# Re-ordering the first five steps of a fused delta-rule and MLP kernel by a new hand-written instruction order

## The chip, the cores and the metric

The kernel runs on one core of a Trainium2 chip. The metric is the device time of one execution in microseconds (us). Inside the core, TensorE (PE, with its weight loads listed apart as PEld), VectorE (DVE), ScalarE (ACT) and GpSimd (POOL) each run their own instructions strictly in the order in which the program issues them, and SyncE (SP) issues nearly all DMAs, also in order.

## The reference

The first part is a delta-rule recurrence over 768 tokens, for 4 batches and 8 heads of width 48; its output is turned into 3072 rows of 384 and goes through an MLP with a hard-swish:

```python
k_n = k / (np.linalg.norm(k, axis=-1, keepdims=True) + 1e-06)
for t in range(S):
    kt, vt, bt = (k_n[:, :, t], v[:, :, t], beta[:, :, t, None])
    y[:, :, t] = np.einsum('bhd,bhde->bhe', q[:, :, t], state)
    v_old = np.einsum('bhde,bhd->bhe', state, kt)
    state = state + bt[:, :, :, None] * np.einsum('bhd,bhe->bhde', kt, vt - v_old)
# x: y as (B*S, H*D) = (3072, 384)
h = x @ w_in                                  # w_in 384 x 2048
g = h * np.clip(h + 3.0, 0.0, 6.0) / 6.0
out = g @ w_out                               # w_out 2048 x 384
```

q, k, v and beta are float32; the two weight matrices are float64 and have to be made float32 on the chip.

## The kernel before

**Tiling.** The 768 tokens are cut into 24 chunks of 32 tokens, called steps 0 to 23; a chunk of all four batches fills 128 partitions. Two steps make one MLP block of 256 rows, so there are 12 blocks. Within a step, the recurrence inside the chunk is solved with the inverse of a triangular 32x32 matrix for each batch and head; between steps a state of 48x48 for each batch and head is carried on. Step 0 gets its inverse by seven small products on PE (`product`); steps 1 to 4 get theirs together by a substitution on DVE (`halves_of`, which loads the matrices in another layout from DRAM and writes the result back through DRAM) and a join on PE (`join`); steps 5 to 8 come from one longer substitution (`inverse`), and so on.

**Weights.** Each matrix is loaded in 8 pieces of 768 KB, 16 pieces in all, as raw float64 words. For each piece ACT computes the exponent in four passes (`scales`, line 335) and DVE builds the float32 in three operations (`convert`, lines 357, 362 and 368). Pieces 1 to 8 are `w_in`, 9 to 16 `w_out`. The raw pieces pass through a few homes, so a late piece waits until an earlier one has been read.

**Steps 0 to 4 and blocks 0 and 1** follow `ORDER`, a text of 822 words. `do` takes one word after the other and issues the next piece of the generator that the word names; this fixes the order on every engine. From step 5 on a loop with a fixed plan issues the rest.

What the words issue:

| word | what one word issues | engine |
|---|---|---|
| `k`, `q`, `v` | one load of 48 KB (one batch of one step) | SP |
| `w` | one raw weight piece, 768 KB | SP |
| `a`; `c` | one of the four ACT passes of a piece; one of its three DVE operations | ACT; DVE |
| `n0` `n1` `n2` `n4` `n5` `n9` | norms of the keys of the steps from that one on (square, sum, root, reciprocals) | ACT, DVE |
| `m`, `b` | beta mask of a step; keys times beta | POOL |
| `p` | preparation of a step, 7 words: scaled keys (POOL), transposes of k (PE), their copy (ACT), transposes of q (PE), their copy (ACT), scores `sc` (PE), masked scores `LB` (DVE) | several |
| `l` | masked scores of a step to DRAM, for the substitution | SP |
| `x0` | the 16 parts of step 0's inverse | PE, DVE, ACT |
| `x1` to `x4` | the 6 parts of a join | several |
| `i1`, `i2` | the substitution of steps 1 to 4 (35 words: load of `A`, 28 DVE operations, a memset, a store, 4 loads back) and of steps 5 to 8 (66 words) | SP, DVE |
| `h` | the chain of a step: state products `ks` (PE), `R` (DVE), `pz` (PE), `Z` (ACT), `su` (PE), new state (DVE); step 0 has only the last four | several |
| `y` | the output of a step: `y`, `py`, `yt`, and at last `xT` (ACT), the MLP's input | several |
| `ua`, `ub` | one of 16 chunks of the up-product of half of block 0 (rows of step 0; of step 1) | PE |
| `ra` `ga`, `rb` `gb`, `ru` `gu` | ACT and DVE part of the hard-swish of such a chunk | ACT, DVE |
| `u` | one unit of MLP work: of every four, two are down-products of block 0 and two are up-products of block 1; the last four are down-products of block 1 | PE |
| `e`, `z`, `s`, `B` | output, settings, pads, beta loads | several |

Four PSUM tiles (`psM`) are shared in turn by `pt`, `pi`, `pz`, `py`, `yt`, `ph` and `po`, so a product waits until the tile four places earlier has been read by ACT or DVE. Two larger ones (`psC`) hold `sc`, `ks` and `su`. There are three `vf` buffers for values, two `kf` buffers for keys (one for a group of four steps) and four for queries.

Below, "the fifth `c`" is the fifth time that this word occurs.

Of the kernel before, what the change touches and what calls it, by code (L numbers as in the profile page):

```python
# [19 lines left out]


ORDER = """
k*2 z k*2 B*2 k B*2 w q s*2 q n0 s q n0 s q z n0 s q s*2 k s z m0 k z*3 n0 k a c m1 k a k c q s a
q*2 n0 n1 n0 q n0 p0 a n1 k*2 b0 p0 n1 c k*2 p0*2 k n1 k n1 p0 n1*2 w p1 n2 p0 w n2 b1 k p1 p0 k*2
x0 p1 m2 p1 k n2 q p1 q n2 x0*2 n2 p1 q a n2 c n2 x0 n2*2 a c p2 a b2 p2 q*2 p3 a q*2 x0 b3 p3 n4
q c p2 q p2 p3 q n4 x0 p2 q c q n4 p2 a n4 w n4*2 p3 n4 w p2 p4 a w x0 w b4 p4 p3 k c x0 p4 m3 k a
k*2 a p1 p4 p3 p4 l2 x0 m4 a c a c a l1 p4 p3 a x0 p4 m5 a c l3 m6 a*2 c a l4 c k x0 c a k*2 x0 n5
k c x0 a k n5 a v x0 a c x0 v c a v x0 a i1 c v a v c w n5 c w a v n5 w c k*2 i1 h0 i1 k i1*2 h0 k
i1*2 y0 i1*3 h0 y0 i1*2 k a y0 i1 c i1 y0 i1 a c a k i1*2 k h0 a i1 h1 a i1 c a k i1 k ua i1 y1 v
c n5 v i1*2 ua ra v y1 a q i1 q i1 ua ga ra q i1 a i1 ua q ga i1*2 q ua ra i1 n5 x1 x2 i1 ra x3 ua  # L30
ga x4 ra q ga n5 ga ua q h1 ra q ua ra q a ua q ga*2 ua q ra n5 ra q ua ra ga i1 ga n5 ua ga ra i1
c a i1 ua i1 ga ua ra c q ra ua ra q a c q k ga a x1 ua k ga*2 x1 ra k x2 ra ga x2 x1 k u x2 x3 k
ga x1 k c k x2 x1 k n5 n9 n5*2 k c v*2 n5 x4 x3 p5 x2 v n9 v h1 p6 x3 n9 v*2 n9 b6 k b5 k w*2 v p5
h1 v n9 v y1 p7 p5 n9 v*2 p6 y1 b7 k*2 c a y1 p8 c h1 y1 b8 p6 p8 a p7 w x3 h1 w a k a k*2 h2 x3 c
k p7 k ub p8 h2 k p8 rb ub y2 k p8 gb c ub rb c a h2 gb rb y2 ub h2 k a gb k ub k ub rb k rb gb h2
v rb gb a gb v k ub h2 a w k ub rb c k ub a k h3 gb k rb c k rb gb a ub v gb c v y2 rb a gb ub y2
w a h3 ub rb ub rb gb v rb gb ub a v gb c ub v rb v h3 rb gb c a ub gb c h3 y2 rb u y2 gb y3 p6 a
y3*2 p6 h3 y3 a y3 h3 p5 y3 q p5 u c q n9 q a c u q c q ru q a gu p5 q n9 q ru p6 p5 a u p6 m7 l5
a gu l6 u a c m8 a p7 u q p7 c q c a q p7 q ru a p8 p7 u p8 m9 l7 n9 c l8 u ru m10 u gu*2 n9*2 u
n9*2 p9 i2 u ru b9 gu p10 p9 ru u b10 p9 gu p9 i2 x4 p9 i2*3 u i2*2 x4 i2 u i2*4 x4 i2 ru i2*2 h4  # L40
x4 gu i2 u y4 i2 h4 u ru i2*2 y4 u i2*2 u gu i2*3 u ru i2 gu i2 u ru i2 gu i2 u i2*3 u i2*3 h4 ru
i2 gu p9 h4 i2*2 y4 p9 u i2 p11 l9 y4 u ru i2 y4 gu u y4 i2*3 u i2*4 u ru i2 gu i2 u ru i2*3 gu u
i2*4 u e i2*2 e*2 i2*3 u ru i2*2 gu i2 h4 ru e gu p10 h4 u p10*2 u p10 u i2*3 p10 u p10 l10
"""


# [1286 lines left out]
```

## Time and profile before

| | |
|---|---|
| median of three runs | 698.09 us (697.37 to 699.77) |
| the profiled execution's own time | 701.2 us |
| its span, first to last instruction | 699.5 us |
| PE busy | 651.9 us, 93% of the span |
| DVE, ACT, POOL busy | 440.0, 240.6, 93.5 us |
| mean granted PE clock | 0.959 of full speed |

The profiled execution took 701.2 us, 1.7 us more than its span and 3.1 us more than the median. A predicted difference is worked out on the profiled execution and then taken from the median.

The page cuts the span in 40 slices of 17.5 us and gives the busy share of each engine in tenths. Above the slices stand the totals; the "chain that ended last" follows the work back from the end; the groups list instructions by line; the list of waits says which engine stood idle until which instruction of another engine was done.

### The profile page before, as it was taken

The page shows a single profiled execution, that of the slowest core. Times are in us where ns is not written, and L with a number is a line of the kernel's source. Part 1 is how long each engine was busy: PE and PEld are TensorE (multiplying, and loading weights), DVE is VectorE, ACT ScalarE, POOL GpSimd, SP SyncE. Part 2 cuts the span into 40 slices and gives each one's busy share as a digit, 9 for nine tenths or more (in the row PEclk, how much of TensorE's full clock was granted, in tenths as well). Part 3 has the DMA queues.
Part 4 walks back from the last instruction along what each step waited for, and adds up shares of the span by engine and source line. Part 5 has one row for each costly group of instructions (what it writes and reads, how often), then busy time and mean ns, then how long its engine had stood idle before and what let it go on. Part 6 is the DMA issues. An engine that isn't in the chain of part 4 may idle for free.

```text
span 699.5 us, 25481 instructions
## 1 busy us (share of the span) xinstructions
PE 651.9 (93%) x11208; PEld 570.9 (82%) x11208; DVE 440.0 (63%) x1174; ACT 240.6 (34%) x476; POOL 93.5 (13%) x146
## 2 busy tenths in 40 slices
PE   2637779999999999999999999999999999999997
PEld 2437669777668998998998998988988989989997
DVE  5678737878545797653796743895544984545342
ACT  5786448722213313313213213223223132132230
POOL 7520110321321010411100401100000000000000
PEclk9857859999999999999999999999999999999999
DMA  6787777401513123414113422015130014000000
GB/s 134 213 195 196 115 210 173 67 33 20 104 39 80 34 43 70 48 39 88 32 29 78 45 45 65 10 42 78 18 70 2 2 36 59 16 11 1 24 0 23
DMA packets 137999, 45.27 MB, mean 65 GB/s; under 512 B 128192, under 2 KB 131264, under 8 KB 137888
## 3 DMA queue, kind: packets, MB, share of 16 engines
q1 hardware_dynamic: 137632, 43.35, 30.3%
q8 instruction: 88, 1.44, 0.9%
q10 hardware_dynamic: 256, 0.30, 0.2%
q14 instruction: 23, 0.19, 0.1%
HBM read 32.87 MB, written 10.75 MB: 62 GB/s over the span
## 4 chain that ended last, share of the span: by engine, by line
PE 81%; DVE 9%; DMA 4%; SPq 3%; issue 2%; ACT 1%; POOL 0%; DVEq 0%
PE ph L946 34%; PE po L1052 23%; PE po L987 6%; PE ks L775 3%; PE pt L474 3%; PE pz L796 3%; PE su L892 2%; PE py L796 2%; PE sc L495 2%; DVE A L724 2%; DVE pr L719 2%; SPq L147 2%; DVE g L1038 1%; DMA qb<-in_q_dram 1%; PE yt L841 1%
## 5 line engine op out<-in xcount | busy, mean ns | idle before, releaser
L946 PE MATMUL ph<-xT,w_in 128*128 128x256 f32 (+1 forms) x1248 | 269.5, 370 | 1.9 <-DVE g L958 1.7
L946 PEld LDWEIGHTS ph<-xT,w_in 128*128 128x128 f32 x1248 | 221.0, 193 | 31.3 <-DVE g L958 2.8
L955 ACT ACTIVATE t<-ph,halves 128x256 f32<-128x256 f32 (+1 forms) x208 | 94.5, 457 | 202.2 <-PE ph L946 201.0
L958 DVE SCALAR_TENSOR_TENSOR g<-t,ph 128x256 f32<-128x256 f32 (+1 forms) x208 | 81.9, 398 | 124.7 <-ACT t L955 124.4
L1052 PE MATMUL po<-w_out,g 128*128 128x192 f32 x640 | 113.3, 328 | 0.0
L1052 PEld LDWEIGHTS po<-w_out,g 128*128 128x128 f32 x640 | 103.8, 190 | 0.5
L1052 PE MATMUL po<-spare,g 128*128 128x192 f32 x480 | 84.8, 330 | 0.0
L1052 PEld LDWEIGHTS po<-spare,g 128*128 128x128 f32 x480 | 78.1, 190 | 1.8
L1038 DVE TENSOR_TENSOR g<-g 128x256 f32<-128x256 f32 x160 | 65.5, 462 | 0.5 <-PE po L1052 0.5
L724 DVE TENSOR_TENSOR A<-A,pr 128x30 f32<-128x30 f32 (+19 forms) x150 | 52.6, 351 | 3.7
L335 ACT ACTIVATE spare<-spare,places 128x768 uint16<-128x768 uint16 (+1 forms) x56 | 52.5, 941 | 4.1 <-DMA qb<-in_q_dram 2.3
L719 DVE TENSOR_TENSOR pr<-A 128x30 f32<-128x30 f32 (+19 forms) x150 | 49.7, 331 | 2.9
L423 POOL TENSOR_TENSOR mb<-beta_tok,mask 128x256 f32<-128x256 f32 x48 | 35.8, 769 | 104.0 <-DVE LB L505 103.9
L987 PE MATMUL po<-w_out,g 128*128 128x384 f32 x128 | 46.4, 501 | 0.0
L1059 ACT ACTIVATE o<-po 128x192 f32<-128x192 f32 x40 | 13.2, 331 | 88.5 <-PE po L1052 82.2
L482 ACT ACTIVATE KQ<-pt 128x512 f32<-128x512 f32 x48 | 28.5, 595 | 31.7 <-PE pt L474 30.4
L458 POOL TENSOR_TENSOR kb<-kf,inv 128x384 f32<-128x384 f32 x24 | 21.3, 888 | 113.4 <-PE pt L474 76.8
L845 ACT ACTIVATE xT<-yt 128x384 f32<-128x384 f32 x24 | 11.7, 488 | 64.7 <-PE yt L841 64.7
L987 PEld LDWEIGHTS po<-w_out,g 128*128 128x128 f32 x128 | 23.4, 192 | 12.6 <-issue 0.5
L474 PE MATMUL pt<-ident,kb 128*128 128x128 f32 x96 | 18.6, 328 | 15.8 <-POOL kb L458 15.8
L775 PEld LDWEIGHTS ks<-state,KQ 64*64 64x64 f32 x1472 | 25.1, 139 | 9.0 <-issue 6.6
L775 PE MATMUL ks<-state,KQ 64*64 64x48 f32 x1472 | 28.4, 225 | 2.5 <-issue 1.4
(104 smaller groups left out, 566.6 us busy)
## 6 DMA issues: line engine op xcount, KB each, us to landing
kf<-in_k_dram SPq DMA_DIRECT2D x96, 48.0 KB, 3.1
qb<-in_q_dram SPq DMA_DIRECT2D x96, 48.0 KB, 2.3
vf<-in_v_dram SPq DMA_DIRECT2D x96, 48.0 KB, 3.1
out_dram<-o SPq DMA_DIRECT2D x92, 48.0 KB, 1.6
spare<-in_moe_w_in_dram SPq DMA_DIRECT2D x4, 768.0 KB, 6.7
w_out<-in_moe_w_in_dram SPq DMA_DIRECT2D x4, 768.0 KB, 7.1
w_out<-in_moe_w_out_dram SPq DMA_DIRECT2D x4, 768.0 KB
spare<-in_moe_w_out_dram SPq DMA_DIRECT2D x4, 768.0 KB, 4.8
```

Of the source, the lines that this page charges most:

```text
L335: nc.scalar.activation(out=z, in_=z if n else d.bitcast(I16)[:, :, :, 3], func=func, bias=places[:, n : n + 1], scale=scale,)
L423: nc.gpsimd.tensor_tensor(out=mb[:, e], in0=beta_tok[:, t, e:H:2].unsqueeze(2).unsqueeze(3).to_broadcast([P, NP, 2, C]), in1=mask2[:].unsq ...
L474: nc.tensor.transpose(pt[:, p, :], src[:, 2 * p : 2 * p + 2].rearrange("p e w -> p (e w)"), ident[:])
L719: nc.vector.tensor_tensor(out=pv, in0=A[:, j, j + 1 :].unsqueeze(1).to_broadcast([n, j, w]), in1=A[:, 0:j, j].unsqueeze(2).to_broadcast([n ...
L724: nc.vector.tensor_tensor(out=A[:, 0:j, j + 1 :], in0=A[:, 0:j, j + 1 :], in1=pv, op=ALU.subtract)
L775: nc.tensor.matmul(ph[y][c, e, D * p : D * p + D], lhsT=KQ[r, p * B // 2 + b // 2, 2 * y : 2 * y + 2, :].rearrange("k y c -> k (y c)"), rh ...
L946: nc.tensor.matmul(ph[:, cols], lhsT=w_in[:, s, f * 128 : (f + 1) * 128], rhs=xT[:, s, cols], start=(s == 0), stop=(s == NKT - 1),)
L955: nc.scalar.activation(out=t1, in_=ph, func=ACTF.Relu, bias=half, scale=1.0 / 6.0)
L958: nc.vector.scalar_tensor_tensor(out=g, in0=t1, scalar=1.0, in1=ph, op0=ALU.min, op1=ALU.mult)
L987: nc.tensor.matmul(pos[c][:], lhsT=gs[blk, f // 2][:, f % 2, c * P : (c + 1) * P], rhs=w_out[:, f, :], start=(f == 0), stop=(f == NFC - 1),)
L1038: nc.vector.tensor_tensor(out=A(f, *out), in0=A(f, *a), in1=A(f, *b), op=op)
L1052: nc.tensor.matmul(ps[n][:], lhsT=A(f - f % 2, *a)[:, f % 2], rhs=b[:, f], start=(f == 0), stop=(f == HF - 1),)
```

## The change

The text `ORDER` is replaced as a whole. Both texts have 822 words, and every word occurs equally often in both, so that the same instructions are issued up to the end of the text and the loop behind it starts from the same point. Only the order differs. What stands elsewhere now:

- Step 0's four value loads: in the queue of SP they were at places 62, 63, 64 and 66, behind the stores for the substitution; they are at places 37, 38, 47 and 52, among the parts of `x0`.
- Weight pieces on SP: piece 2 from place 27 to 17, pieces 3 to 8 from 28, 45, 46, 47, 48, 68 to 26, 32, 41, 48, 50, 54; pieces 11 to 16 from 121, 122, 130, 131, 146, 154 to 73, 79, 90, 105, 121, 135. Piece 11 had 49 key loads in front of it and now has 28; piece 16 had all 68 and now has 52.
- The four stores `l` and the load of `A` (`i1`) are now directly one behind the other on SP (places 55 to 59; before 53 to 56 and 65).
- Block 0 (numbers of words in the text): the `ua` words run from 232 to 369 (before 282 to 380), the `ub` words from 384 to 495 (before 478 to 576). `ua` now starts ahead of step 0's state update, and the first `ga` comes behind 25 of the 35 words of `i1` (as before) without `c` words between.
- Step 1's `h1` and `y1` stand at 313 to 382 (before 274 to 465), ahead of the norms of later steps.
- The `u` words start at 518 (before 393); `m`, `b`, `s` words on POOL and the early `n` words are spread anew. On DVE step 0's norm now comes ahead of the first `c`.

```diff
@@ -20,27 +20,27 @@


 ORDER = """
-k*2 z k*2 B*2 k B*2 w q s*2 q n0 s q n0 s q z n0 s q s*2 k s z m0 k z*3 n0 k a c m1 k a k c q s a
-q*2 n0 n1 n0 q n0 p0 a n1 k*2 b0 p0 n1 c k*2 p0*2 k n1 k n1 p0 n1*2 w p1 n2 p0 w n2 b1 k p1 p0 k*2
-x0 p1 m2 p1 k n2 q p1 q n2 x0*2 n2 p1 q a n2 c n2 x0 n2*2 a c p2 a b2 p2 q*2 p3 a q*2 x0 b3 p3 n4
-q c p2 q p2 p3 q n4 x0 p2 q c q n4 p2 a n4 w n4*2 p3 n4 w p2 p4 a w x0 w b4 p4 p3 k c x0 p4 m3 k a
-k*2 a p1 p4 p3 p4 l2 x0 m4 a c a c a l1 p4 p3 a x0 p4 m5 a c l3 m6 a*2 c a l4 c k x0 c a k*2 x0 n5
-k c x0 a k n5 a v x0 a c x0 v c a v x0 a i1 c v a v c w n5 c w a v n5 w c k*2 i1 h0 i1 k i1*2 h0 k
-i1*2 y0 i1*3 h0 y0 i1*2 k a y0 i1 c i1 y0 i1 a c a k i1*2 k h0 a i1 h1 a i1 c a k i1 k ua i1 y1 v
-c n5 v i1*2 ua ra v y1 a q i1 q i1 ua ga ra q i1 a i1 ua q ga i1*2 q ua ra i1 n5 x1 x2 i1 ra x3 ua
-ga x4 ra q ga n5 ga ua q h1 ra q ua ra q a ua q ga*2 ua q ra n5 ra q ua ra ga i1 ga n5 ua ga ra i1
-c a i1 ua i1 ga ua ra c q ra ua ra q a c q k ga a x1 ua k ga*2 x1 ra k x2 ra ga x2 x1 k u x2 x3 k
-ga x1 k c k x2 x1 k n5 n9 n5*2 k c v*2 n5 x4 x3 p5 x2 v n9 v h1 p6 x3 n9 v*2 n9 b6 k b5 k w*2 v p5
-h1 v n9 v y1 p7 p5 n9 v*2 p6 y1 b7 k*2 c a y1 p8 c h1 y1 b8 p6 p8 a p7 w x3 h1 w a k a k*2 h2 x3 c
-k p7 k ub p8 h2 k p8 rb ub y2 k p8 gb c ub rb c a h2 gb rb y2 ub h2 k a gb k ub k ub rb k rb gb h2
-v rb gb a gb v k ub h2 a w k ub rb c k ub a k h3 gb k rb c k rb gb a ub v gb c v y2 rb a gb ub y2
-w a h3 ub rb ub rb gb v rb gb ub a v gb c ub v rb v h3 rb gb c a ub gb c h3 y2 rb u y2 gb y3 p6 a
-y3*2 p6 h3 y3 a y3 h3 p5 y3 q p5 u c q n9 q a c u q c q ru q a gu p5 q n9 q ru p6 p5 a u p6 m7 l5
-a gu l6 u a c m8 a p7 u q p7 c q c a q p7 q ru a p8 p7 u p8 m9 l7 n9 c l8 u ru m10 u gu*2 n9*2 u
-n9*2 p9 i2 u ru b9 gu p10 p9 ru u b10 p9 gu p9 i2 x4 p9 i2*3 u i2*2 x4 i2 u i2*4 x4 i2 ru i2*2 h4
-x4 gu i2 u y4 i2 h4 u ru i2*2 y4 u i2*2 u gu i2*3 u ru i2 gu i2 u ru i2 gu i2 u i2*3 u i2*3 h4 ru
-i2 gu p9 h4 i2*2 y4 p9 u i2 p11 l9 y4 u ru i2 y4 gu u y4 i2*3 u i2*4 u ru i2 gu i2 u ru i2*3 gu u
-i2*4 u e i2*2 e*2 i2*3 u ru i2*2 gu i2 h4 ru e gu p10 h4 u p10*2 u p10 u i2*3 p10 u p10 l10
+k*4 B*4 w s n0 k*2 n0 z*2 s k n0*2 z n0 k z n1 n0*2 q z a*3 p0 m0 k*2 q n1*2 q c k q s c n1 w p0 a
+p0*3 k a k n2 k*2 q z s k*2 q p0 w n1*2 a c n1 p0 s q a p1 x0 n2*2 a n2 s x0 n2 x0*2 k a n2 a*2
+n2*2 p1 n2 q*3 a m1 c w k x0*2 c q s k c x0 b0 p1 a q p1 a p2 v x0 c p1 a c x0 c*3 v q x0 n4*2 p2
+k x0 p2*2 p1 w b1 a b2 m2 c q n4 q*3 p2 q c*2 p1 v x0 w n4*3 p3 a*2 n4 p2 m3 p3 a*2 q p3 p4 x0 a w
+p3 p4 a p2 c p3 q p4 x0 p4*2 a*3 m4 v p3 a k c p4 p3 p4 w c*2 a c x0*2 h0 a c a l1 l2 a c l3 h0 l4
+a*2 c y0 i1 k y0 v b3 y0 c*2 k y0 w ua*2 w i1 ra i1*4 ua i1*7 a i1 k i1*7 a i1*2 k v ra i1*2 a ga
+i1 h0 i1 ra ua i1 ua i1 ra i1 ga ua ga*2 ra c ga ra k ga h0 ua ra ga k ua n5 a ra v ga ua a ra c
+ua v ra i1 ga*2 c a ua h1 ua*2 n5 x1 w ra*2 ua ga i1 x1 ga c x1 v k x1 x2 k x1 n5 ra n5 i1 ga a*2
+h1 x1 c m5 w ua c v h1 ra y1 h1 x3 y1*2 a h1 ga i1 k*2 a v c a*2 h1 y1 ua ra a n5 x2 k h2 y1 k x2
+n5 b4 c y1 ga ub*2 ra k ga q k n5 x2 w ub rb n5 a n5 v n5 k rb x2 gb y2 n5*2 gb rb x2 q ub rb n5
+h2 ub gb rb i1 q gb p5 gb k p6 s h2 v ub rb k p5 h2 p5 ub x3*2 q y2 q k v b5 b6 x4 x3 gb k n9 q
+ub*3 rb w rb*2 gb*2 c a v gb ub y2 ub k y2 h2 rb gb rb gb v rb a*2 v n9 gb h2 x3*2 ub p5 q rb ub c
+ub p5 p7 gb y2 ub rb*2 h3 gb*2 c v p6 a k a y2 h3 p8 k y3 p6 k rb gb k n9 u q y3 p7 h3 q k n9 p7
+h3 p8*2 a c k q y3*2 p6 c y3 u y3 a p6 c m6 w q u c a ru h3 a n9 gu x4 h3 a u k q ru q k c q*2 a v
+k q a u q u gu n9 p5 v c k p6 a p7 w p7 u n9 p6 ru p5 v*2 n9 m7 v b8 a gu u p8 n9 p8 m8 p7 c p8 q
+ru p7 n9 s u a p8 u b7 q u l5 a gu k u n9 a u ru n9*2 v c gu q u p9*2 c h4 ru c gu q l6 a p9 c*3 v
+x4*2 u l8 ru h4 u p10 gu l7 y4 k m9 m10 y4 p10 q u q p10 q u i2*2 ru i2*4 k gu p10 x4 p10 v x4 p9
+i2 p9 i2 q u*2 i2 v i2*2 v i2*2 ru i2*4 k i2*3 gu i2 u h4 i2*2 ru i2*4 p9 h4 p9 p10*2 i2 u*2 k gu
+ru u*2 i2*3 q i2 gu i2*4 k u i2 u i2 ru gu u b10 u i2 ru i2*9 q ru k u gu u l10 e h4 e y4 u i2*2
+gu i2*2 k i2 ru i2 l9 i2 q i2 ru i2 u i2 u i2*3 k i2 k b9 k p11 h4 k y4 k*4 e i2 y4 gu e i2*3 u*2
+gu y4
 """


```

## The prediction

> **What bounds the kernel now.** I read the 40 slices first, then the busy time by stages, then the waits and the order of time of the stages that are not full.
>
> ```profile
> PE   2637779999999999999999999999999999999997
> DVE  5678737878545797653796743895544984545342
> ACT  5786448722213313313213213223223132132230
> PEclk9857859999999999999999999999999999999999
> DMA  6787777401513123414113422015130014000000
> ```
>
> PE is full from the seventh slice (105 us) to the end; before it, it is half empty, the clock falls to half twice, and DMA is at 70 to 80%. So a new order can gain only before 105 us. The stages, cut where the first `ua` product, the first `ub` product and step 5's first `ks` start:
>
> ```profile
> core 0: us, PE busy (x) PEld busy (x) DVE busy (x) ACT busy (x) POOL busy (x), PEclk, DMA share, GB/s
> 0.00:63.16 63.16, 28.97 (x1003) 23.80 (x1004) 43.16 (x108) 43.49 (x62) 26.98 (x62) 0.75 0.79 194
> 63.16:102.36 39.20, 31.22 (x760) 26.49 (x760) 22.93 (x66) 20.43 (x42) 6.76 (x9) 0.72 0.70 143
> 102.36:120.38 18.02, 18.02 (x418) 16.95 (x415) 13.44 (x35) 14.95 (x29) 0.00 (x0) 0.88 0.76 188
> 120.38:183.46 63.08, 62.94 (x1120) 46.53 (x1112) 46.37 (x117) 26.04 (x47) 12.74 (x16) 1.00 0.29 57
> 183.46:699.50 516.04, 510.78 (x7922) 457.12 (x7921) 314.09 (x854) 135.69 (x298) 47.02 (x59) 1.00 0.22 40
> ```
>
> Step 5 begins at 183.46 us, where the text is used up. The last row, 516 us, is the same program before and after. The text's own PE work at full clock, from warm rows: 32 half chunks `ph` x 0.76 (90 matmuls in 11.44 us are 15 of them) = 24.3; 16 full `ph` x 1.30 = 20.8; 20 down units x 1.29 = 25.8; 11 preparations x (0.43 + 0.43 + 0.80) = 18.3; steps, 4 `ks` x 1.08 + 15 `pz`, `py`, `su` x 0.81 + 5 `yt` x 0.33 = 18.1; products and joins about 10.7. Sum 118 us. So **65 us of the 183.5 are lost**: by the same sum over the words done, 45.4 before `ua` starts (17.7 of work), 16.3 more before `ub` (40.6 of work at 102.4), 4 after it. What is waited for:
>
> ```profile
> PE pz L796 <- DMA vf<-in_v_dram: 3.3, 3, 1.4
> ACT sq L386 <- DMA kf<-in_k_dram: 7.0, 2, 5.3
> DVE ss L392 <- ACT sq L386: 6.3, 1, 6.3
> ```
>
> The first is of 49 to 63 us, the others of 63 to 102 us: step 0's values come late, and keys of steps 5 to 12 hold up ACT and, behind it, DVE. SP issues all of this in line:
>
> ```profile
> 28.36 1.52 SPq L310 DMA_DIRECT2D w_out<-in_moe_w_in_dram  x3
> ...
> 35.88 7.04 SPq L446 DMA_DIRECT2D l_dram<-LB  x4
> ...
> 53.55 9.74 SPq L147 DMA_DIRECT2D kf<-in_k_dram  x9
> ```
>
> Weight pieces 4 to 6 go out only at 28 us, the four stores hold the queue for 7 us, and nine key loads take 9.7 us.
>
> [...] so a load behind `l` or `i1` waits for them; the four `l` issues above agree. [...] a key issue took 0.5 to 1.1 us. Fewer of them ahead of the weights is relief.
>
> **The change part by part.** All counts are equal, so only waits count.
>
> *Start.* DVE does step 0's norm ahead of the first conversion: keys scaled at about 8.7 instead of 11.15 us. But q's fourth load is sixteenth on SP instead of tenth: it lands near 13 to 14, and the first `LB` stays at 16 to 17 (before 15.98). Nothing gained.
>
> *Weights and `x0`.* At about 0.6 us an issue, piece 2 goes out at 10 (before 14.8), 4 at 19 (28.4), 8 at 35 (50.3), landing 5 to 7 us later, as now. ACT is then the bound. Along its new order, with 0.95 for a pass, 0.60 for a copy, 0.52 for a square: passes 5 to 8 from 15.6, first copy in `x0` at 21.5, passes 9 to 15 and two copies, second copy in `x0` at 31 (before 43.6), `p4`'s last copy at 41.6, pass 24 at 43.5. DVE's c 17 to 19 and the last part of `x0` follow: 46.4 (before 49.0). Values went out by 33 and are there, so `pz` does not wait until 53.4 as now. ACT takes six more passes first (`Z` at 49.7), then two, `y`, `xT`: **`ua` starts at 54** without a stall. Before, ACT stood still some 5 us between 20 and 49; I take 3 for this: **57** (before 63.2).
>
> *Substitution and `ua`.* The four `l` wait for the last `LB` (43.5; before about 40), hold SP, and `i1` right behind them waits for their landing (5 us in the trace): `A` goes out at 49 and lands at 53.4, as now (48.75, 53.17). Queued behind: k, v 5, pieces 9 and 10, which go out near 51 as now. DVE runs 24 substitution operations at 0.27 = 6.5 us ahead of the first `ga`; until then four PSUM tiles fill and PE stands still, about 57 to 60. Its store then holds SP from about 55 to 62, with piece 11 behind it, which still leaves 30 us earlier than now (90.6). Two trips through DRAM (4 + 4.3, as at 68.6 to 77.7) give the first join at 71 and step 1's `pz` at 75 (before 85.9), the state at 79, `xT` behind seven ACT operations at 82.5. **`ub` starts at 84** without a stall. In this stretch DVE has 25.6 us of work in 30 us, more than it has done anywhere here; I add 4: **88** (before 102.4). Norms of steps 5 to 8 no longer stand before step 1's output, which takes out the 6.3 us DVE wait; late next is ACT's pass 45 on piece 12, and k of step 9 (out 79 to 87, needed near 90).
>
> *`ub` to the end.* Text work done at `ub` is then 35.6, so 82.4 remain (before 77.4 in 81.1). DVE has 67.9 and ACT 48 of it, SP about 100 issues of 0.5: all beside PE. Piece 16 goes out later and has 5 to 7 us to land before its pass is due, with up to 2 us of wait to be absorbed by four PSUM tiles; on DVE the long substitution is packed, but I find 6.7 us of DVE between the last `gu` it needs and `y4`, against 9.4 us on PE. Keys 60 to 68 come behind outputs and `q`; step 5 wants them on POOL only. POOL's masks and scaled keys total 33 us of 105 and lie beside. Loss 6 (before 4).
>
> **Sum:** 88 + 82.4 + 6 = 176.4, against 183.5: 7.1 us less. Profiled execution 701.2 - 7.1 = 694.1; the median of the runs is 3.1 lower: **691.0**.
>
> [...] It has "issue" gaps, one of 5.44 us at 32.4 us while three pieces were in flight. [...] Spread pieces could take away up to 5 us, or gaps in a denser stream add 5; I take 0 and keep both ends.
>
> **The rivals.**
> - *No stalls:* `ub` at 84, the end with 4 of loss: 170.4, 13 us less, **685**. For it: less DMA ahead of it. Against it: no stretch before 105 us has run without waits.
> - *DVE takes over:* substitution, conversion and hard-swish meet between 57 and 88; if DVE is busy for no more than its present share (22.93 + 13.44 in 57.2 us is 0.64), 25.6 us need 40, `ub` comes at 97, and half a microsecond stays: **697.5**. For it: DVE in order, with waits on all others.
> - *Slower: the block on SP.* The load of `A` is directly behind the stores, and nothing can fill PE between the fourth `ua` and the first `ga`. Whatever delays `p4`'s `LB` (planned 43.5) moves `A`, the inverses, step 1 and `ub` one to one. `ub` must be at 97.5 to lose nothing (35.6 + 61.8), so it decides from an `LB` near 53. For it: 22 ACT passes now stand ahead of it, before 12, and pieces 5 and 6 must land in time. With 58, ub at 102.5: 5 us more, **703**.
> - *Hidden anyway:* no; PE has 42 us of idle time before 105, and no count differs, so the change does what it says.
>
> **The numbers.** Forecast 0.50, no stalls 0.13, DVE 0.17, block 0.20. About 0.3% (2 us) is what a measurement of this kernel can tell. The forecast's own range is 684 to 695, all faster, as is the second case; the third is faster for 0.03, equal for 0.12, slower for 0.02; the fourth slower. That gives 0.66, 0.12 and 0.22. The range from 683 to 701 leaves out a little of the second and more than half of the fourth.
>
> **What would show it.** Right: `ua` starting at 54 to 60 and `ub` at 84 to 92, `pz` of step 0 without a wait for `vf`, no ACT wait of 5 us for `kf`, step 5's `ks` near 176, the rest 516 long. Wrong: `l` issued after 50, DVE without idle time while PE waits for `g`, a first `ga` after 66, or a stage behind step 5 that is longer than 516.

## The result and the profile after

The changed kernel takes **693.91 us** (median of 20 runs, 691.1 to 698.6), the kernel before 698.48 us (20 runs, 696.3 to 701.4). The ratio is **0.9932, 95% interval 0.9916 to 0.9948**: 4.6 us less, and outside the 0.3% that can be told from no change. Forecast were 691.0 us, 7.1 us less. The profiled execution of the changed kernel took 691.84 us, 2.1 us less than the median, with a span of 690.1 us.

The page's slices, 17.25 us each:

```profile
PE   1659799999999999999999999999999999999997
DVE  5878656788535985834985734984544984445242
ACT  5886558522133223232233232232222132132230
PEclk9967799999999999999999999999999999999999
DMA  7987746513614126024025122025020014000000
```

PE is full from the sixth slice (86 us) on, before from the seventh (105 us). The clock, which before fell to 0.5 in the third and in the sixth slice, is at 0.6 to 0.7 in slices three to five and full behind them. The stages, cut where the first `ua`, the first `ub` and step 5's first `ks` start (wall time, then busy time and count by engine, granted clock, DMA share, GB/s):

```profile
core 0: us, PE busy (x) PEld busy (x) DVE busy (x) ACT busy (x) POOL busy (x), PEclk, DMA share, GB/s
0.00:54.41 54.41, 26.04 (x876) 20.67 (x876) 38.76 (x90) 40.83 (x58) 26.10 (x58) 0.83 0.84 201
54.41:84.63 30.22, 25.98 (x675) 23.80 (x675) 22.30 (x66) 19.11 (x36) 0.00 (x0) 0.75 0.75 180
84.63:174.01 89.38, 85.40 (x1752) 66.31 (x1740) 66.68 (x168) 44.37 (x85) 24.19 (x32) 1.00 0.44 94
174.01:690.10 516.09, 510.81 (x7922) 457.23 (x7921) 312.36 (x851) 135.50 (x298) 44.90 (x57) 1.00 0.22 40
```

The last row is again 516.1 us, as it is in all 14 profiles of this study (516.0 to 516.2). So everything lies ahead of step 5, as forecast. What step 0's values and the queue look like now, first on PE, then on SP (start, duration, operation, count, idle time before it and what ended it):

```profile
48.18 1.50 PE L796 MATMUL pz<-vf,LB 32*32 32x48 f32 x64 [1.66 <-DVE LB L605]
54.41 4.21 PE L946 MATMUL ph<-xT,w_in 128*128 128x128 f32 x18 [0.58 <-ACT xT L845]
58.55 1.14 PE L892 MATMUL su<-Z,bkb 32*64 32x48 f32 x64
59.62 6.14 PE L946 MATMUL ph<-xT,w_in 128*128 128x128 f32 x48
```

```profile
19.12 0.45 SPq L310 DMA_DIRECT2D w_out<-in_moe_w_in_dram  x1
...
36.53 8.80 SPq L446 DMA_DIRECT2D l_dram<-LB  x4
47.95 0.34 SPq L671 DMA_DIRECT2D A<-l_dram  x1
...
61.30 0.35 SPq L693 DMA_DIRECT2D x_dram<-A  x1
```

Step 0's `pz` starts as one piece and waits for the inverse (`LB`), no longer for `vf`; `ua` follows 6.2 us later. Piece 4 goes out at 19.12 us (before 28.4), `A` at 47.95, the substitution's store at 61.30. ACT's wait of 7.0 us for `kf` is gone. In 54 to 105 us its largest is for its own input `ph` (us in total, times, longest):

```profile
ACT t L955 <- PE ph L946: 10.1, 13, 1.7
```

### The profile page after: what moved, and what is told of

Same layout as the page of the kernel before. It is cut to its first block, busy times and chain, and to the rows that moved or that the text cites. A ratio compares the mean times of both kernels' runs of the same rounds, so it can differ in the third digit from the quotient of the medians.

```text
span 690.1 us, 25473 instructions
## 1 busy us (share of the span) xinstructions
PE 648.2 (94%) x11208; PEld 568.0 (82%) x11208; DVE 440.1 (64%) x1174; ACT 239.8 (35%) x476; POOL 95.2 (14%) x146
## 3 DMA queue, kind: packets, MB, share of 16 engines
q8 instruction: 88, 1.44, 0.9%
## 4 chain that ended last, share of the span: by engine, by line
PE 78%; DVE 11%; DMA 6%; issue 2%; ACT 2%; SPq 1%; DVEq 0%
PE ph L946 33%; PE po L1052 23%; PE po L987 6%; PE ks L775 3%; PE pz L796 3%; PE py L796 3%; PE su L892 2%; DVE A L724 2%; PE pt L474 2%; DMA w_out<-in_moe_w_in_dram 2%; PE sc L495 2%; DVE pr L719 2%; DMA spare<-in_moe_w_in_dram 2%; DVE g L1038 1%; ACT spare L335 1%
## 5 line engine op out<-in xcount | busy, mean ns | idle before, releaser
L987 PE MATMUL po<-w_out,g 128*128 128x384 f32 x128 | 44.8, 490 | 0.0
L907 DVE TENSOR_TENSOR state<-state,su 128x384 f32<-128x384 f32 x46 | 23.3, 547 | 14.7 <-PE su L892 14.7
L788 DVE SCALAR_TENSOR_TENSOR y<-ks,parity,y 128x192 f32<-128x192 f32 x46 | 17.0, 410 | 18.4 <-ACT y L812 18.3
```

What stands on the lines that cost most here:

```text
L987: nc.tensor.matmul(pos[c][:], lhsT=gs[blk, f // 2][:, f % 2, c * P : (c + 1) * P], rhs=w_out[:, f, :], start=(f == 0), stop=(f == NFC - 1),)
```

## The experiments

The stage times of all profiles in us. "ub" is the end of step 1's `xT`, from which `ub` can start; "sub" is the first operation of the substitution.

| kernel | sub | `ua` | step 1 `pz` | ub | step 5 `ks` | median, us | ratio to before (95%) |
|---|---|---|---|---|---|---|---|
| before, first profile | 53.2 | 63.2 | 85.9 | 97.9 | 183.5 | 698.5 | |
| before_again | 55.4 | 65.2 | 87.2 | 96.4 | 181.8 | | |
| changed, first profile | 53.4 | 54.4 | 73.3 | 84.6 | 174.0 | 693.9 | 0.9932 (0.9916–0.9948) |
| after_again | 54.1 | 55.1 | 75.0 | 85.4 | 176.0 | 693.5 | 0.9907 (0.9879–0.9934) |
| s1_new_then_old | 58.4 | 65.7 | 86.9 | 96.5 | 181.7 | 700.3 | 1.0015 (1.0002–1.0028) |
| s1_old_then_new | 53.5 | 63.4 | 77.7 | 90.6 | 181.4 | 698.8 | 0.9991 (0.9975–1.0006) |
| v_late | 56.6 | 57.7 | 76.8 | 88.2 | 180.6 | 697.8 | 0.9979 (0.9965–0.9993) |
| v_early | 52.9 | 63.1 | 85.8 | 98.2 | 183.4 | 698.9 | 0.9982 (0.9968–0.9997) |
| keys_first | 52.4 | 53.4 | 82.3 | 93.4 | 183.5 | 702.1 | 1.0052 (1.0033–1.0070) |
| ua_behind_ks | 54.8 | 62.1 | 78.8 | 91.3 | 182.4 | 697.4 | 0.9971 (0.9952–0.9989) |
| w_late | 67.2 | 68.2 | 87.2 | 98.2 | 188.3 | 706.1 | 1.0087 (1.0068–1.0105) |
| imp1 | 52.2 | 53.1 | 72.9 | 82.8 | 173.1 | 691.3 | 0.9883 (0.9863–0.9904) |
| imp2 | 64.3 | 57.8 | 84.5 | 99.0 | 197.4 | 714.9 | 1.0200 (1.0177–1.0224) |
| imp3 | 53.6 | 54.6 | 73.9 | 85.2 | 174.7 | 693.7 | 0.9935 (0.9920–0.9950) |

In the diffs below, words are those of `ORDER`; "`w` 4" is the fourth `w`. Each is written as the order of the queue that it changes.

### Both kernels a second time

Nothing is edited.

> The changed kernel once more, for the spread between executions and a second profile. Theory (the new order brings step 5's first ks forward by about 9 us in the profile, and the rest of it is scatter between executions): ua at 54 to 57 us, ub at 84 to 88, step 5's first ks at 173 to 178, ratio 0.991 to 0.995. Rival (the 9.4 us between the two profiles are the true gain and the 20 timed runs hide it): ratio near 0.987.

> The kernel before once more, for a second profile. Theory (the profiled execution of before was an unlucky one, 2.5 us over the median, and the unlucky part lies ahead of step 5): step 5's first ks at 180 to 182 us, not 183.5, and 516 us behind it. Rival (the offset lies in the loop behind step 5 or outside the span): ks at 183 to 184, and less than 516 behind it.

Measured: the changed kernel's second profile has step 5's `ks` at 176.04 us, 2.0 later than the first; that of before has it at 181.84, 1.6 earlier. One profile of each would say 9.5 us of gain, the other 5.8; the medians say 4.6. In before_again the loads of step 0's values are again what `pz` waits for (58 of its 64 matmuls start at 55.77 us, after 2.34 us of waiting for `vf`). So the pattern repeats and the size of it doesn't: stage times of single profiles are good to about 2 us, and what follows is read with that.

### One half of the order each

```diff
 s1_new_then_old: ORDER = new text's first 232 words (all ahead of the first ua)
-  + rest of the new text
+  + the words left over, in the order of the old text
 s1_old_then_new: ORDER = old text's first 282 words (all ahead of the first ua)
-  + rest of the old text
+  + the words left over, in the order of the new text
```

> The new order up to the first ua product, then all words that are left in the order of before. Theory (both stretches gain by themselves: 9 us up to ua, 9 us between ua and ub, of which 5 are PE work that before had done earlier): ua at 54 to 57, then 36 to 39 us to ub as before, ub at 91 to 95, half of the gain: ratio 0.994 to 0.998. Rival (the start is hidden anyway behind the substitution and step 1): ub near 100 and ratio 0.998 to 1.002. Second rival (the start makes all of it): ub at 84 to 88, ratio 0.991 to 0.994.

> The order of before up to the first ua product, then all words that are left in the new order. Theory (both stretches gain): ua at 61 to 64, then some 30 us to ub, ub at 91 to 95, ratio 0.995 to 0.999. Rival (the start makes all of it): ub near 100, ratio 0.998 to 1.003. Second rival (the start is hidden anyway): ub at 84 to 88.

Neither half gives anything, 1.0015 and 0.9991, where some half of the gain was expected of each. Both cuts fall ahead of the first `ua`, and in both kernels PE still has step 1's `ks` in front of `ua`, as before. With the new start alone, PE shows what that does:

```profile
52.39 0.90 PE L841 MATMUL yt<-ident,y 128*128 128x128 f32 x3 [0.67 <-ACT y L829]
53.22 1.24 PE L892 MATMUL su<-Z,bkb 32*64 32x48 f32 x64
63.36 2.41 PE L775 MATMUL ks<-state,KQ 64*64 64x48 f32 x64 [8.91 <-DVE state L907]
65.70 4.49 PE L946 MATMUL ph<-xT,w_in 128*128 128x128 f32 x31
```

Step 0's output is as early as in the changed kernel (`yt` at 52.4, there 52.9). But in the old order step 1's `ks` stands ahead of `ua` on PE, waits for step 0's state, and DVE makes that only from 62.76 us, in the midst of the substitution. That in turn started 5.0 us late, behind two key norms that waited 1.49 and 2.96 us for ACT's squares. **Here the early output brings nothing, because `ks` stands in front of `ua`.** With the old start and the new rest, `ua` stays at 63.4. Step 1's `pz` is 8.2 us and `ub` 7.3 us earlier than before, but 5 us of that are order only: in the new rest less PE work has been done when `ub` starts (the prediction's 82.4 us remain, against 77.4). Step 5's `ks` is 2.1 us earlier than in the first profile of before and 0.4 us earlier than in the second, and the time of the runs shows nothing.

### Step 0's values: late in the new order, early in the old

```diff
 SP queue, v_late (changed kernel)      SP queue, v_early (kernel before)
- v 1, v 2, v 3, v 4 (places 37 to 52)  + v 1, v 2, v 3, v 4
  l1 l2 l3 l4, i1 (load of A)             w 4
+ v 1, v 2, v 3, v 4                      ...
  k 23                                  - v 1, v 2, v 3, v 4 (places 62 to 66)
```

> The changed kernel with step 0's four value loads put back behind the stores and the load of A on SP, all other engines as changed. Theory (the values were worth the 3 to 4 us for which pz waited for them): they go out near 49 us, land at 52 to 54, pz of step 0 starts 4 to 6 us later than 48.2, ua at 58 to 60, the loads of A unchanged, ratio to before 0.995 to 1.000. Rival (pz's wait is covered by the substitution, which holds up the first ga until 60 anyway): ua later but ub within 1 us of 84.7, ratio 0.991 to 0.995.

> The kernel before with only step 0's four value loads moved ahead of weight piece 4 on SP. Theory (in the order of before ua stands behind step 0's new state and step 1's ks, and the state behind the substitution on DVE, so an earlier pz finds no use): pz of step 0 without a wait for vf, xT of step 0 some 4 us earlier than 58.9, but ua still at 61 to 64 and the ratio 0.997 to 1.002. Rival (the values alone are the 4 us that the changed kernel lost with late values): ua at 58 to 60, ratio 0.993 to 0.996.

v_late: the four loads go out from 47.82 us and `pz` starts at 51.37, after 5.01 us of idle PE. The row names a DVE conversion as releaser; the values' time to landing, 2.9 to 3.4 us, fits better. `ua` and the substitution come 3.3 and 3.2 us later, the end 3.3 us (0.9979 against 0.9932, times 699). That this would be hidden behind the substitution is refuted, and DVE's last row ahead of it says how:

```profile
55.75 0.96 DVE L367 SCALAR_TENSOR_TENSOR w_in<-spare 128x768 f32<-128x768 f32 x1 [4.49 <-ACT spare L334]
```

The last conversion in front of the substitution waits 4.49 us for an ACT pass that stands behind `Z`, and `Z` waits for `pz`. Late values hold the substitution through passes and conversions that don't read them.

v_early, the same part alone in the old order, gives 0.9982, within what can be told from no change, though `pz` no longer waits for values (49.01 us). Step 0's `xT`, expected some 4 us earlier, ends at 59.24 us where it ended at 59.42 before: ACT has the first pass on the last `w_in` piece in front of it, and waits for that piece. On PE `ks` stands in front of `ua` again. First ACT, then PE:

```profile
57.87 1.00 ACT L335 ACTIVATE spare<-spare,places 128x768 uint16<-128x768 int16 x1 [3.42 <-DMA spare<-in_moe_w_in_dram]
58.76 0.48 ACT L845 ACTIVATE xT<-yt 128x384 f32<-128x384 f32 x1
```

```profile
60.75 2.41 PE L775 MATMUL ks<-state,KQ 64*64 64x48 f32 x64 [4.85 <-DVE state L907]
63.09 11.45 PE L946 MATMUL ph<-xT,w_in 128*128 128x128 f32 x90
```

### `ua` behind step 1's `ks` again

```diff
 PE, changed kernel
+ h0 3 (su of step 0), h1 1 (ks of step 1)
  ua 1
  ...
- h0 3, h1 1
 DVE: h0 4 (new state) behind the 17th i1
```

> The changed kernel with step 0's su and step 1's ks ahead of the first ua product on PE, and the new state in the midst of the substitution on DVE, as before; loads, ACT and POOL as changed. Theory (the early values pay only because ua no longer waits for state and ks): ua at 60 to 63 instead of 54.4, step 1's pz within 2 us of 73 to 75 since it hangs on the substitution, ub 2 to 6 us later because the ua products are then missing as a filling, ratio to before 0.996 to 1.002. Rival (the substitution sets everything and ua only fills gaps): ub within 1 us of 84.6, ratio 0.991 to 0.995.

```profile
59.78 2.41 PE L773 MATMUL ks<-state,KQ 64*64 64x48 f32 x64 [3.37 <-DVE state L905]
```

`ks` waits 3.37 us for the state and starts at 59.78; `ua` at 62.1 instead of 54.4. Of these 7.7 us, 6.7 are left at `ub` and 2.7 in the time (0.9971 against 0.9932). The profile overstates it: its execution, 700.2 us, was the slowest of the 14, whose median is 697.4. Step 1's `pz`, expected within 2 us of 73 to 75, came at 78.8: the substitution started 1.4 us later and had the new state in its midst, and its store went out at 65.43 instead of 61.30. "Block 0 ahead of the state" is thus a part without which more than half of the gain is lost. It isn't enough by itself: v_late above and the two kernels below keep it and lose most of the gain or all of it. No run has it alone in the old order.

### Late keys ahead of the substitution's store

```diff
 SP queue, changed kernel
  v 8
+ k 29 to k 49 (21 loads)
  i1 31 (store of the inverses)
  w 11
- k 29 to k 49, spread over the next 60 places
```

> The changed kernel with 21 key loads (steps 7 to 12) put ahead of the substitution's store on SP, and so ahead of weight pieces 11 and later, as before. Theory (the keys cost their issue time where the store and the loads back of the inverses stand behind them): 21 issues of 0.5 to 1.1 us fill SP from 55 to between 66 and 78, the store goes out 5 to 15 us later than 61.3, step 1's pz and ub follow by as much, ratio to before 1.000 to 1.015. Rival (SP stands idle from 55 to 61 anyway, and PE has ua products to fill): at most 3 us later, ratio 0.993 to 0.998.

```profile
57.98 11.14 SPq L145 DMA_DIRECT2D kf<-in_k_dram  x21
69.22 0.39 SPq L691 DMA_DIRECT2D x_dram<-A  x1
```

21 loads take 11.14 us, 0.53 us each, of SP's time, and the store goes out 7.9 us later than in the changed kernel. Then on PE, with all that is ahead of the first join done:

```profile
65.75 2.27 PE L944 MATMUL ph<-xT,w_in 128*128 128x128 f32 x18
77.70 1.05 PE L631 MATMUL pi<-LB,VY 16*32 16x16 f32 x64 [9.68 <-DVE VY L641]
```

PE stands still for 9.68 us, `ub` can start 8.8 us later, and the time is 8.4 us longer (1.0052 against 0.9932): longer than before the change. So a block on SP passes on nearly one to one: 7.9 us at the store, 8.8 at `ub`, 8.4 in the time. The slower rival's own block, a late `LB` ahead of the load of `A`, is a stage earlier on the same way and was not made here.

### Weight pieces late again

```diff
 SP queue, changed kernel
- w 4 (ahead of k 19), w 5 (ahead of q 14)
  v 3
- w 6, q 19, w 7, q 20, v 4, k 22, w 8
+ q 19, q 20, w 4, w 5, w 6, w 7, v 4, k 22
  l1 l2 l3 l4, i1 (load of A)
+ w 8
```

> The changed kernel with weight pieces 4 to 7 behind all 20 query loads of steps 0 to 4 and piece 8 behind the load of A on SP, about where the kernel before had them. Theory (an ACT fed late is what held ua at 63): pieces 4 to 7 go out near 31 to 33 instead of 19 to 34, ACT waits 3 to 6 us for piece 4, pz of step 0 and ua 2 to 5 us later, ub as much, ratio to before 0.994 to 1.000. Rival (the queries, sooner by four pieces, bring step 4's scores and the substitution forward, and ua only waits for pieces): ub within 1.5 us of 84.6, ratio 0.989 to 0.994.

ACT's rows show the two waits (`spare<-w_out` and `spare<-spare` are first passes over a raw piece):

```profile
35.26 1.01 ACT L334 ACTIVATE spare<-w_out,places 128x768 uint16<-128x768 int16 x1 [9.82 <-DMA w_out<-in_moe_w_in_dram]
...
62.18 1.97 ACT L334 ACTIVATE spare<-spare,places 128x768 uint16<-128x768 int16 x2 [7.12 <-DMA spare<-in_moe_w_in_dram]
```

`A` goes out at 54.30 us, 6.4 later. The substitution is later by 13.8, since DVE has the conversion of the late piece 8 in front of it:

```profile
62.19 0.56 DVE L356 TENSOR_SCALAR spare<-spare 128x768 uint32<-128x768 uint32 x1 [5.36 <-DMA spare<-in_moe_w_in_dram]
62.79 0.96 DVE L361 SCALAR_TENSOR_TENSOR spare<-spare 128x768 f32<-128x768 uint32 x1
66.35 0.96 DVE L367 SCALAR_TENSOR_TENSOR w_in<-spare 128x768 f32<-128x768 f32 x1 [2.60 <-ACT spare L334]
```

From there it is passed on one to one: `ua` is 13.8 us later, `ub` 13.6, step 5's `ks` 14.3, and the time 1.55% (10.8 us) longer than the changed kernel's. Expected were 2 to 5 us, from ACT's first wait; the second, for piece 8, was not counted. Of the parts tried this is the costliest to set back. Its price is an upper one: piece 4 leaves here at 29.5 us (before the change 28.4), but piece 8 at 54.7 (50.3).

### Three attempts at a faster version

The first has its edit on SP alone: `qb`, for which PE waited 1.84 us at 41.6 us in the changed kernel, is loaded ahead of two weight pieces.

```diff
 SP queue, changed kernel
  v 3
+ q 19, q 20
  w 6
- q 19
  w 7
- q 20
```

> The changed kernel with the last two query loads of step 4 ahead of weight piece 6 on SP; nothing else moved. In the changed kernel PE waited 1.84 us for that load, and step 4's masked scores, the stores and the load of A hang on it. Theory (the chain from step 4's scores through the substitution sets ub one to one): the substitution starts 1.5 to 2.5 us earlier than 53.4 to 54.1, ub 1 to 2 us earlier than 84.6 to 85.4, ratio to before 0.987 to 0.992. Rival (pieces 6 to 8 come later by as much and hold ACT and DVE instead): pz of step 0 and ua 1 us later, ratio 0.991 to 0.996.

That wait is gone, `ub` comes 1.9 us earlier than in the first profile of the changed kernel, as expected, and imp1 has the lowest time of all: 691.28 us, 0.9883 (4 runs). What PE now waits for ahead of step 0's `pz` has no releaser in the profile:

```profile
42.37 1.03 PE L494 MATMUL sc<-KQ 64*32 64x64 f32 x80 [1.10 <-issue]
43.33 0.60 PE L544 MATMUL pi<-VY 32*32 32x32 f32 x47
46.29 0.44 PE L544 MATMUL pi<-VY 32*32 32x32 f32 x17 [2.36 <-issue]
```

The second attempt:

```diff
 changed kernel with imp1's edit, and besides:
  DVE, ACT, POOL: products of step 0's inverse and preparations of
  steps 3 and 4 ahead of conversions and passes
```

> As imp1, and besides: step 4's norm, the masked scores and the parts of step 0's inverse go ahead of conversions on DVE, the last key and query copies ahead of five ACT passes, step 0's Z, y and xT ahead of four to six, step 3's and 4's scaled keys ahead of the masks on POOL. Theory (conversions are ahead of need: the first ua products need one piece, not eight): pz of step 0 at 42 to 46, ua at 47 to 52, substitution from 49 to 53, ub at 79 to 83, ratio 0.983 to 0.990. Rival (ACT's 64 passes are the bound up to ub, so that what moves ahead comes back as a wait of ua for its piece): ua early, ub at 84 to 87, ratio 0.990 to 0.995.

It is slower, 714.88 us (1.0200, 1.0177 to 1.0224). In its text step 3's scaled keys (the 127th word) come into the buffer that they share with step 1's before step 1's have been transposed (the 133rd), so step 1's scores are made from step 3's keys, with the same amount of work. PE's transposes for step 1 wait 7.1 us for these, and POOL waits 10.4 us for step 4's norm in front of step 4's scaled keys and the masks behind them. The row on PE, and POOL's wait (us in total, times, longest):

```profile
26.46 1.12 PE L471 MATMUL pt<-ident,kb 128*128 128x128 f32 x4 [7.14 <-POOL kb L455]
POOL kb L455 <- DVE inv L407: 11.4, 2, 10.4
```

The order that it meant to try was therefore not tried, and nothing is taken from it on the change.

The third attempt:

```diff
 changed kernel with imp1's edit, and besides:
 DVE:  n4 4 to 7, p1 7, x0 12 ahead of the twelfth c
 ACT:  p3 5, p4 3, p4 5 ahead of the 21st a
```

> imp1, and besides on DVE the end of step 4's norm, step 1's masked scores and one part of step 0's inverse ahead of piece 4's conversion, and on ACT the last three copies of steps 3 and 4 ahead of pass 21, which waits for piece 6. Theory (step 4's scores set the substitution, and it sets ub): masked scores of step 4 some 2 us earlier than 43.5, substitution at 50 to 51.5 instead of 52.2, ub at 81 to 82.3 instead of 82.8, step 5's first ks at 171 to 173, ratio 0.984 to 0.988. Rival (PE's issue gaps of 1.1 and 2.4 us at 42 to 46 us set the scores, not the order): substitution within 0.5 us of 52.2, ratio 0.987 to 0.991.

No gain beyond the change: 693.66 us, 0.9935. The rows that answer to imp1's:

```profile
42.68 1.03 PE L494 MATMUL sc<-KQ 64*32 64x64 f32 x80 [1.58 <-issue]
43.64 0.60 PE L544 MATMUL pi<-VY 32*32 32x32 f32 x47
47.42 0.44 PE L544 MATMUL pi<-VY 32*32 32x32 f32 x17 [3.18 <-issue]
```

The scores and the last product of step 0's inverse start when PE's own gap of 1.58 and 3.18 us ends, not when DVE is ready, so an earlier DVE brings nothing. The substitution at 53.64 us and the ratio lie outside the ranges of theory and rival alike: the gaps themselves are 0.5 and 0.8 us longer than in imp1. Nor is imp1's lead settled by this: its interval lies below the changed kernel's first one, but overlaps with that of after_again, and imp3 has the same loads in the same places. That `qb` is off PE's path in imp1 is shown; that it is worth 2 to 3 us is not.

## Why the prediction was right, and where not

- **What bounds it, and where gain is possible: right.** PE ahead of step 5; the rest is 516.1.
- **Start and weights: right.** Scaled keys and first `LB` came at 9.7 and 16.1 us (said: 8.7 and 16 to 17), pieces 2, 4 and 8 went out at 10.7, 19.1 and 36.0 us (10, 19, 35). Of the parts tried, w_late shows it as the most costly to set back.
- **`ua`: right in time, not in the reason.** It started at 54.4 and 55.1 us, where 54 without and 57 with stalls were said. ACT's waits were there all the same: 3.9 us in 20 to 49 us in the first profile and 4.6 in the second, against 5.3 before. They lay on the way: from its last wait at 42.3 us to `Z` ACT never stood still. So the plan without stalls was too long by about as much as the waits took, and that its 54 fits is in part luck. (The second copy in `x0` came at 30.4, where 31 was said, and `Z` at 50.2, where 49.7 was said.)
- **"PE stands still, about 57 to 60": wrong.** PE took 4.21 us for the first 18 matmuls of `ua`, 234 ns each where the warm rows of before have 127, and then had `su`. The granted clock was 0.50 in 54.4 to 58.6 us, so slow work stood where the idle time was expected. The first `ga` came at 60.07, as said.
- **SP's block: right.** `A` out at 47.95 (49), store 61.3 (62), first join 69.5 (71), step 1's `pz` 73.3 and 75.0 (75). SP issued nothing from 45.3 to 47.95 and from 55.2 to 61.30 us, ahead of `A` and of the store, with loads standing behind each of them.
- **DVE's 4 us ahead of `ub`: too much.** DVE was busy for 22.30 of 30.22 us, 0.74, where the rival "DVE takes over" had it end at 0.64. `ub` could start at 84.6 and 85.4, said were 88.
- **Loss behind `ub`: too little.** 89.38 us for 82.4 of work are 7.0, and 8.2 in the second profile, against 6.
- **The sum.** In the new order 15.8 us of work come ahead of `ua` (17.7 before, which had `su` and `ks` among them: 1.9 by the forecast's prices), and 35.6 ahead of `ub`. The lost time, 118 us of work taken off, is then 38.6 + 10.4 + 7.0 = 56.0 us in the first profile and 58.0 in the second, where the forecast had 41.2 + 11.2 + 6 = 58.4. Its end on an execution, 176.4 + 516.0 + 1.7 = 694.1 us, is 0.2 from the measured median. That is in part luck: 2.6 to 3.4 us too much up to `ub` were in part set off by 1.0 to 2.2 too little behind it.
- **The step that failed** is the last, "the median of the runs is 3.1 lower"; the mechanism was right in the main, and this term was mis-sized. That the first profile of before lies 3 us above its median is a property of that execution, not of the kernel: the second has step 5's `ks` 1.6 us earlier, and an ordinary execution (698.5 less 1.7 and 516.1) has it at 180.7. The new stages were added up from ordinary durations, so there was nothing to take off: 180.7 - 176.4 = 4.3, and 4.6 were measured. The gain of 7.1 was mis-sized by a third for that reason.
- **Rivals.** "No stalls" was right up to `ub` (84) and then lost 3 to 4 us more than it assumed. "Slower" did not come, since `LB` of step 4 left in time; keys_first and w_late show what blocks of its kind cost.
- **What was not foreseen: the parts are not a sum.** By ratio, setting back values, the place of `ua`, keys and weights one at a time costs 3.3, 2.7, 8.4 and 10.8 us (each ratio less 0.9932, times 699), together 25 us where the whole gain is 4.6. Keys and weights were set back further than they had been before, so the sum is an upper one. The halves point the same way, but weakly: with `ua` behind `ks` as before, the new start and the new rest together still gain 2.0 us (ua_behind_ks), and each for itself 0.6 us or less (s1_old_then_new, s1_new_then_old); that difference is little more than what can be told from no change. The reading of these runs is that the parts stand on one path, where one left late holds the rest, as the late piece in front of `xT` in v_early does.

## What to carry to other kernels

When an order is written by hand over in-order engines, its parts are a chain and not a sum: look for the instruction that stands ahead of the early work on each engine (here `ks` ahead of `ua`, 8.91 us of idle PE; keys ahead of a store, which went out 7.9 us later; a pass on a late piece ahead of `Z`, 7.12 us of idle ACT), since here one of them left in place took more than half of the gain, or all of it. Build the new end from ordinary durations and compare it with an ordinary execution of the kernel before, not with the one that was profiled: two profiles of one kernel differed by 1.6 to 2.0 us in the stage that mattered. In a new order the first thing to save is what the queue's transfers are for: 21 small loads ahead of one store cost 8.4 us.

## What the runs showed of the hardware

- **PE's gaps without a releaser lay 127 recorded matmuls apart.** In imp1 and imp3 a gap named "issue" lies behind 48 of 128 `sc`, and the next 80 `sc` and 47 `pi` later, that is 127 recorded matmuls. In the two profiles of before one lies behind 49 `sc`, and the next 79 `sc` and 48 `pi` later. The page of the changed kernel has a DMA queue named for instructions (packets, MB, share):

```profile
q8 instruction: 88, 1.44, 0.9%
```

  88 packets of together 1.44 MB are 16.4 KB each, one for every 127 of PE's 11208 matmuls. In the first profile of before one packet of this queue falls into each of 35.5 to 36.0, 40.5 to 41.0 and 59.5 to 60.0 us, and gaps end at 37.88, 43.08 and 62.35; the packet in 26.0 to 26.5 us has no such gap behind it. Ahead of 60 us single gaps took up to 1.5 us in the changed kernel, 3.2 in imp3 and 5.4 before. The equal distance and these times speak for PE waiting for these packets; no run tested it, and what delays them is not shown.
- **These gaps are a rival that no run separates.** Ahead of `ua` they add up to 9.7 and 9.8 us in the two profiles of before, and to 2.0 and 1.7 us in those of the changed kernel. The forecast set this term at nothing, with 5 us either way. How much of the earlier `ua` comes from shorter gaps stays open. They don't explain the price of late weights: w_late has 1.95 us of them ahead of `ua`, and loses 10.8 us.
- **The clock was low without a long idle stretch.** Between 44 and 58.5 us of the changed kernel's first profile the granted clock was 0.50, though from 30 us on PE had never stood still for over 1.9 us; it was busy for 5.3 of the 10.4 us ahead of `ua`. These are the rows (as in the table of stages):

```profile
44.00:48.00 4.00, 1.37 (x74) 1.03 (x64) 3.67 (x6) 3.90 (x5) 1.19 (x2) 0.50 0.53 74
48.00:54.41 6.41, 3.91 (x132) 3.14 (x132) 5.66 (x11) 5.30 (x8) 1.43 (x2) 0.50 0.81 257
54.41:58.55 4.14, 4.14 (x19) 3.92 (x19) 3.66 (x15) 2.42 (x5) 0.00 (x0) 0.50 0.87 234
```

  In the second profile, again without a pause over 1.9 us from 30 us on, `pz` at 49.0 and `py` at 51.5 us took 1.50 us for 64 matmuls each, as they did in the first at a clock of 0.50; step 5's `pz` at 181.3 us of the first, at a clock of 1.00, took 0.88. In the first profile of before the two longest stretches at 0.50 began at 34.8 us, 2.4 us into a pause of PE of 5.44, and at 86.0, where between 63.2 and 86.0 PE had never stood still for over 2.1 us. A long pause thus goes with the first of them and not with the second; what lowers the clock is not shown.
